# The old state of a gated linear attention joins the new product through an identity matmul on TensorE instead of an addition on VectorE

## The chip, the cores and the metric

The kernel runs on one core of a Trainium2 chip. The metric is the device time of one execution in microseconds (us); the number given is the median of several executions.

## What is computed

Three layers follow each other. The first is a gated linear attention with a 48 x 48 state for each of 4 x 8 heads over 768 positions. The second sends each of the 3072 tokens to one of eight experts, if its skip score is positive. The third is a three-way maximum of products and an output product.

```
for t in range(S):                       # S = 768, state is 48 x 48 for each head
    state = alpha[:, :, t, :, None] * state + einsum('bhd,bhe->bhde', k[:, :, t], v[:, :, t])
    y[:, :, t] = einsum('bhd,bhde->bhe', q[:, :, t], state)
...
x[do_compute] += gate * (relu(x @ w1[e]) @ w2[e])      # one expert e per token
...
out = max(x @ w1, x @ w2, x @ w3) @ w_out
```

Only the first layer is touched by the change.

## The kernel before

The first layer works on chunks of 128 positions: 4 batches of 6 chunks, 24 chunks in all, with all 8 heads of a batch at once (4 pairs of heads, two heads of a pair in the two halves of the 128 partitions). The loop at line 491 takes one chunk a pass; below, **step n** is its pass for chunk n, and c is the number of the chunk in its batch (0 to 5). The rest of the program (the experts and the third layer, from about 145 us on) follows the loop and is not changed.

One step holds, for TensorE (PE) in this order: `scores(n+1)` (line 265, 8 matmuls with operands of 64 partitions), `trans(n+1)` (line 256, 4 transposes), `rows(n-1)` (line 316, 4 matmuls), then `outs(n)`: 4 matmuls of the old state with the queries (line 303, tile `bd`, only for c > 0) and 8 of the masked scores with the values (line 306, a stationary operand of 64 columns); last `upd(n)` (line 283, 8 matmuls of keys and values with a stationary operand of 64 columns, tile `pu`). All are in float32, and each such matmul appears in the trace as two instructions. `trans` and `upd` do nothing for the last chunk of a batch (c = 5), so `trans` is missing in the step with c = 4 and `upd` in the step with c = 5.

VectorE (DVE) does in one step: two scans for chunk n+3 (lines 222 and 236, with a small reciprocal at 230 between them), two masks for chunk n+1 (line 271, tiles `ps` to `sm`), a small reduction of the logits of chunk n-1 (line 324), and the update of the state: `pu + w` (line 290, for c > 0) and the product with the decay (line 291; line 288 for c = 0), which writes the new `w`. After the last chunk of a batch come the routing instructions of that batch: lines 358 to 377 in the next step with c = 0, lines 390 to 413 two steps later.

ScalarE (ACT) then copies `w` into the block-diagonal `bd` (lines 294 and 295), which the next step's line 303 reads. GpSimd (POOL) multiplies keys and queries by the scans' results (lines 225 and 240) and issues the scatters of routed tokens (line 416); its order is fixed too. DMAs are issued by SyncE (SP).

Each engine runs its instructions in the order in which the program writes them. `ps`, `pu`, `py`, `px` and `pk` have one buffer each in PSUM (two tiles for `ps`), so `scores(n+2)` must wait for the masks of chunk n+1, and the update on VectorE must wait for the end of line 283 of its own step. Neither engine can therefore get a whole step ahead of the other.

Of the kernel before, what the change touches and what calls it, by code (L numbers as in the profile page):

```python
# [15 lines left out]
ALU = mybir.AluOpType  # L16
# [4 lines left out]
NP = H // 2  # L21
# [60 lines left out]
def tile_gla_moe_moe2(ctx, tc, akq, vp, rp, wgt, cst, io, ew, md, out):  # L82
    nc = tc.nc
    V, A, G, T, SY = nc.vector, nc.scalar, nc.gpsimd, nc.tensor, nc.sync
# [35 lines left out]
    with tc.manual_schedule():  # L120
        cs = const.tile([128, 3 * 128 + NTILE + 8], F32, name="cs")
        rps = const.tile([PR, NP, 105], F32, name="rps")
        ident = cs[:, 0:128]
# [125 lines left out]
        fr, kks, yts, wt, xr, lg = {}, {}, {}, {}, {}, {}  # L249
# [24 lines left out]
        def upd(j):  # L274
            b, c = seq[j]
            if c == NC - 1:
                return
            kk = kks.pop(j)
            pu = ps_u.tile([128, 512], F32, name="pu")[:, 0:NP * D].rearrange("p (a d) -> p a d", a=NP)
            for p in range(NP):  # L280
                for i in range(2):
                    r0 = 64 * i
                    T.matmul(pu[r0:r0 + 64, p, :], kk[:, p, r0:r0 + 64], vt[j][:, (2 * p + i) * D:(2 * p + i + 1) * D],
                             start=True, stop=True)
            w = wk.tile([PR, NP, D], F32, name="w")
            tb = totm[:, b, :, c + 1:c + 2].to_broadcast([PR, NP, D])
            if c == 0:
                V.tensor_tensor(w, pu, tb, ALU.mult)
            else:
                V.tensor_tensor(pu, pu, wt[b, c], ALU.add)  # L290
                V.tensor_tensor(w, pu, tb, ALU.mult)
            wt[b, c + 1] = w
            t = bd[(c + 1) % 2]
            A.copy(t[0:64, :, 0:D], w[0:64])
            A.copy(t[64:PR, :, 64:64 + D], w[64:PR])
# [195 lines left out]
        for n, (b, c) in enumerate(seq):  # L491
# [10 lines left out]
            low_part = rows(n - 1) if n else None  # L502
            outs(n)
            upd(n)
            if n > nseq - 4:
                low_part()
# [51 lines left out]
        for k in range(k3):  # L558
            for m in range(2):
                T.matmul(acc[k][:, m * 128:(m + 1) * 128], xe[:, m, k * 128:(k + 1) * 128], ident,  # L560
                         start=False, stop=False)
# [244 lines left out]
        tb = [big(f"tb{i}") for i in range(5)]  # L806
# [318 lines left out]
        for s in range(2):  # L1125
# [9 lines left out]
            for j in range(8):  # L1135
                if s == 1 and j == 7:
                    break
                n, c = 1 - j // 4, j % 4
# [226 lines left out]
```

## Time and profile before

| | |
|---|---|
| median of 3 executions | 592.22 us (592.09 to 594.73) |
| the profiled execution | 592.59 us, span 590.8 us |
| TensorE busy, matmuls | 563.1 us (95% of the span) |
| VectorE busy | 440.9 us (75%) |
| ScalarE busy | 297.8 us (50%) |
| GpSimd busy | 247.5 us (42%) |
| mean granted TensorE clock | 0.998 of 2.4 GHz |
| loop of the 24 chunks | from about 7 us to 135 us |

The span runs from the first to the last instruction; 1.8 us of the profiled execution's time lie around it. The shares are means over the whole program and hide the loop, in which VectorE is nearly as busy as TensorE. So the loop is read from its own stretches, from the waits in it, and from the order of instructions in time, whose rows give the start of a group, how long it lasts until its last instruction ends, and after a "<-" whom it waited for. A matmul takes longer from its start to its end than the next one needs to follow it, so prices of matmuls are read from one group's start to the next one's start.

### The profile page before, as it was taken

What the parts mean: (1) busy time and instruction counts of PE and PEld (TensorE: products, weight loads), DVE (VectorE), ACT (ScalarE), POOL (GpSimd) and SP (SyncE); (2) the same over time, 40 slices, a digit from 0 to 9 for tenths busy, and PEclk for the clock granted to TensorE, in tenths of its full rate; (3) what the DMA queues carried; (4) which work ended last, traced back from release to release, by engine and by line L of the source; (5) the groups of instructions that cost most, each with busy time, mean ns of one, the idle gap of its engine ahead of it and who ended that gap; (6) DMA issues with size and microseconds to landing.
All of it is one profiled execution on the core that took longest, in us unless ns stands there. A gap on an engine that the chain in (4) does not pass through costs nothing.

```text
span 590.8 us, 10710 instructions
## 1 busy us (share of the span) xinstructions
PE 563.1 (95%) x3995; PEld 502.8 (85%) x3995; DVE 440.9 (75%) x747; ACT 297.8 (50%) x602; POOL 247.5 (42%) x202
## 2 busy tenths in 40 slices
PE   6999999999999989999999998899999999999995
PEld 3888888888899989999988887788787899887895
DVE  7999999977788898888769895493766674766700
ACT  3656575654576665665333444355354375454310
POOL 5554598653365445654122022122364400455410
PEclk9999999999999999999999999999999999999999
DMA  8889898925787879884419149307464571355011
GB/s 314 323 252 340 288 305 312 347 97 186 255 276 281 303 227 329 260 306 153 161 35 287 37 153 373 144 11 283 138 234 163 199 256 53 134 199 202 0 56 59
DMA packets 50973, 123.04 MB, mean 208 GB/s; under 512 B 4546, under 2 KB 38832, under 8 KB 47328
## 3 DMA queue, kind: packets, MB, share of 16 engines
q1 hardware_dynamic: 44512, 112.13, 55.4%
q10 hardware_dynamic: 3840, 5.31, 2.6%
q0 software_dynamic: 2560, 4.83, 2.2%
q8 instruction: 33, 0.54, 0.4%
q14 instruction: 28, 0.23, 0.1%
HBM read 93.03 MB, written 32.28 MB: 212 GB/s over the span
## 4 chain that ended last, share of the span: by engine, by line
PE 55%; DVE 13%; issue 5%; ACT 4%; DMA 3%; POOL 1%; ACTq 0%; DVEq 0%; POOLq 0%
PE po L1001 3%; PE po L1002 3%; PE po L1003 3%; PE ph L1001 3%; PE ph L1002 3%; PE ph L1003 3%; PE ph L658 2%; PE ph L659 2%; PE po L678 2%; PE po L676 2%; PE po L677 2%; PE ph L660 2%; DVE wl L118 2%; DVE hf L855 2%; PE po L1071 2%
## 5 line engine op out<-in xcount | busy, mean ns | idle before, releaser
L118 POOL TENSOR_TENSOR wl<-raw,wh 128x768 fp32r<-128x768 f32 x26 | 49.2, 1893 | 63.9 <-ACT wh L117 63.8
L118 DVE TENSOR_TENSOR wl<-raw,wh 128x768 fp32r<-128x768 f32 x38 | 57.2, 1506 | 11.6 <-ACT wh L117 11.6
L117 ACT CAST wh<-raw 128x768 fp32r<-128x768 f32 x64 | 53.5, 836 | 21.8 <-PE po L678 10.7
L658 PE MATMUL ph<-xh,wh 128*128 128x256 f32 x192 | 56.5, 294 | 3.7 <-DVE hl L664 3.5
L659 PE MATMUL ph<-xl,wh 128*128 128x256 f32 x192 | 54.5, 284 | 0.4 <-DVE xl L118 0.3
L660 PE MATMUL ph<-xh,wl 128*128 128x256 f32 x192 | 54.4, 283 | 0.0
L676 PE MATMUL po<-wh,hh 128*128 128x384 f32 x128 | 43.5, 340 | 0.0
L678 PE MATMUL po<-wh,hl 128*128 128x384 f32 x128 | 43.3, 338 | 0.0
L677 PE MATMUL po<-wl,hh 128*128 128x384 f32 x128 | 43.2, 337 | 0.0
L658 PEld LDWEIGHTS ph<-xh,wh 128*128 128x128 f32 x192 | 36.5, 190 | 5.3 <-DVE hl L664 5.1
L265 PE MATMUL ps<-q,k 64*128 64x128 f32 x384 | 31.7, 286 | 9.3 <-POOL q L240 5.5
L225 POOL TENSOR_TENSOR k<-akq,sf 128x512 f32<-128x512 f32 x24 | 28.5, 1188 | 23.0 <-DVE sf L222 14.5
L265 PEld LDWEIGHTS ps<-q,k 64*128 64x128 f32 x384 | 26.0, 187 | 13.7 <-POOL q L240 6.9
L659 PEld LDWEIGHTS ph<-xl,wh 128*128 128x128 f32 x192 | 36.4, 190 | 0.8 <-DVE xl L118 0.8
L660 PEld LDWEIGHTS ph<-xh,wl 128*128 128x128 f32 x192 | 36.4, 189 | 0.0
L416 POOL DMA_INDIRECT slots<-xr,si x24 | 24.4, 1015 | 27.8 <-DVE xr L413 11.9
L664 DVE SCALAR_TENSOR_TENSOR hl<-ph,hh 128x256 fp32r<-128x256 f32 x64 | 26.5, 417 | 9.4 <-ACT hh L663 9.3
L663 ACT ACTIVATE hh<-ph 128x256 fp32r<-128x256 f32 x64 | 24.7, 386 | 14.9 <-PE ph L660 13.6
L236 DVE TENSOR_TENSOR_SCAN ap<-akq,pcs 128x521 f32<-128x521 f32 x24 | 29.8, 1241 | 2.2
L222 DVE TENSOR_TENSOR_SCAN sf<-akq,pcs 128x520 f32<-128x520 f32 x24 | 29.4, 1225 | 2.4 <-DMA akq<-in_akq_dram 2.1
L271 DVE TENSOR_TENSOR sm<-ps,cs 128x512 f32<-128x512 f32 x48 | 30.3, 674 | 0.5 <-PE ps L265 0.5
L240 POOL TENSOR_TENSOR q<-akq,ap 128x512 f32<-128x512 f32 x24 | 28.4, 1185 | 5.2 <-DVE ap L236 2.9
(659 smaller groups left out, 1722.3 us busy)
## 6 DMA issues: line engine op xcount, KB each, us to landing
raw<-in_ew_dram SPq DMA_DIRECT2D x15, 1536.0 KB, 6.8
akq<-in_akq_dram SPq DMA_DIRECT2D x22, 772.5 KB, 7.2
rm<-in_md_dram SPq DMA_DIRECT2D x12, 768.0 KB, 7.6
mh<-wd SPq DMA_DIRECT2D x7, 1024.0 KB, 5.1
ml<-wd SPq DMA_DIRECT2D x7, 896.0 KB, 6.7
raw<-wd SPq DMA_DIRECT2D x6, 1024.0 KB, 5.1
raw<-wd SPq DMA_DIRECT2D x6, 896.0 KB, 6.7
vt<-in_vp_dram SPq DMA_DIRECT2D x24, 200.0 KB, 7.0
```

Of the source, the lines that this page charges most:

```text
L117: A.copy(h, src)
L118: (eng or V).tensor_tensor(l, src, h.bitcast(F32), ALU.subtract)
L265: T.matmul(ps[i][:, p, :], kh[j][r0:r0 + 64, p, :], qh[j][r0:r0 + 64, p, :], start=True, stop=True)
L658: T.matmul(ph, wh[:, z], xh_[e][:, k, :], start=(k == 0), stop=False)
L659: T.matmul(ph, wh[:, z], xl_[e][:, k, :], start=False, stop=False)
L660: T.matmul(ph, wl[:, z], xh_[e][:, k, :], start=False, stop=(k == k3 - 1))
L676: T.matmul(po, hh[:, zm], wh, start=(f == 0), stop=False)
L677: T.matmul(po, hh[:, zm], wl, start=False, stop=False)
L678: T.matmul(po, hl[:, zm], wh, start=False, stop=(f == nf1 - 1))
L1001: T.matmul(bk, uh, vh, start=start, stop=False, skip_group_check=not start)
L1002: T.matmul(bk, uh, vl, stop=False, **more)
L1003: T.matmul(bk, ul, vh, stop=True, **more)
```

## The change

In `upd`, for c > 0, the old state `wt[b, c]` (128 partitions x 192 columns, float32) is multiplied by the 128 x 128 identity into `pu` first, with `start=True`. The eight products of keys and values then accumulate on it, each with `start=False`. VectorE's addition is left out; its product with the decay reads `pu` as before. Sixteen of the 24 steps have c from 1 to 4 and are changed; in the four steps with c = 0 and the four with c = 5 the same instructions run as before. No other instruction changes its place on any engine.

```diff
             pu = ps_u.tile([128, 512], F32, name="pu")[:, 0:NP * D].rearrange("p (a d) -> p a d", a=NP)
+            if c:
+                T.matmul(pu, ident, wt[b, c], start=True, stop=False)
             for p in range(NP):
                 for i in range(2):
                     r0 = 64 * i
                     T.matmul(pu[r0:r0 + 64, p, :], kk[:, p, r0:r0 + 64], vt[j][:, (2 * p + i) * D:(2 * p + i + 1) * D],
-                             start=True, stop=True)
+                             start=(c == 0), stop=(c == 0 or p == NP - 1))
             w = wk.tile([PR, NP, D], F32, name="w")
             tb = totm[:, b, :, c + 1:c + 2].to_broadcast([PR, NP, D])
-            if c == 0:
-                V.tensor_tensor(w, pu, tb, ALU.mult)
-            else:
-                V.tensor_tensor(pu, pu, wt[b, c], ALU.add)
-                V.tensor_tensor(w, pu, tb, ALU.mult)
+            V.tensor_tensor(w, pu, tb, ALU.mult)
             wt[b, c + 1] = w
```

## Rows read from the trace of the kernel before

**Rows 1.** Windows: busy us (x instructions) of PE, PEld, DVE, ACT, POOL; PEclk, DMA share, GB/s.

```profile
95.00:110.00 15.00, 14.55 (x187) 13.40 (x189) 14.40 (x28) 8.27 (x22) 13.31 (x13) 1.00 0.83 287
145.00:592.00 447.00, 430.11 (x2378) 384.68 (x2377) 313.92 (x460) 217.27 (x391) 160.59 (x109) 1.00 0.53 184
```

**Rows 2.** Waits, 14 to 131 us: line waited for, total us, times, longest us.

```profile
PE ps L265 <- DVE sm L271: 3.3, 5, 0.9
PE ps L265 <- POOL q L240: 1.5, 3, 0.7
...
DVE pu L290 <- PE pu L283: 4.1, 7, 1.3
```

**Rows 3.** Order in time, PE, steps 3 to 5: start us, length us, group.

```profile
27.39 1.16 PE L265 MATMUL ps<-q,k 64*128 64x128 f32 x16
...
28.97 1.04 PE L316 MATMUL px<-rps,yt 128*128 128x105 f32 x8
29.84 1.08 PE L303 MATMUL py<-q,bd 128*128 128x128 f32 x8
30.85 1.09 PE L306 MATMUL py<-sm,vt 128*64 128x128 f32 x16
31.77 0.62 PE L283 MATMUL pu<-vt,kk 128*64 128x48 f32 x16
32.33 1.16 PE L265 MATMUL ps<-q,k 64*128 64x128 f32 x16
33.42 1.14 PE L316 MATMUL px<-rps,yt 128*128 128x105 f32 x8
34.39 1.08 PE L303 MATMUL py<-q,bd 128*128 128x128 f32 x8
...
41.53 1.09 PE L306 MATMUL py<-sm,vt 128*64 128x128 f32 x16
42.55 1.25 PE L265 MATMUL ps<-q,k 64*128 64x128 f32 x16
```

**Rows 4.** Order in time, weight loads (PEld) of step 3.

```profile
30.85 0.85 PEld L306 LDWEIGHTS py<-sm,vt 128*64 128x64 f32 x16
31.67 0.60 PEld L283 LDWEIGHTS pu<-vt,kk 128*64 128x64 f32 x16
```

**Rows 5.** Order in time, PE: matmuls with wide moving operands after the loop.

```profile
139.29 0.61 PE L560 MATMUL pk<-cs,xe 128*128 128x128 f32 x4
139.74 0.61 PE L560 MATMUL pu<-cs,xe 128*128 128x128 f32 x4
...
201.19 0.34 PE L676 MATMUL po<-wh,hh 128*128 128x384 f32 x1
201.37 0.34 PE L677 MATMUL po<-wl,hh 128*128 128x384 f32 x1
```

**Rows 6.** Order in time, DVE: a step that DVE sets, and its parts.

```profile
95.77 0.19 DVE L324 TENSOR_REDUCE pcs<-px 128x9 f32<-128x36 f32 x1
95.87 0.35 DVE L290 TENSOR_TENSOR pu<-pu,w 128x192 f32<-128x192 f32 x1
96.26 0.36 DVE L291 TENSOR_TENSOR w<-pu,totm 128x192 f32<-128x192 f32 x1
...
100.42 0.20 DVE L324 TENSOR_REDUCE pcs<-px 128x9 f32<-128x36 f32 x1
```

**Rows 7.** Order in time, DVE: first and next instruction around both routing parts.

```profile
47.06 0.20 DVE L358 TENSOR_REDUCE mx<-pcs 128x6 f32<-128x48 f32 x1
...
48.98 1.21 DVE L222 TENSOR_TENSOR_SCAN sf<-akq,pcs 128x520 f32<-128x520 f32 x1
...
58.71 0.22 DVE L390 TENSOR_TENSOR rk<-pr,om 128x48 f32<-128x48 f32 x1
...
60.30 1.21 DVE L222 TENSOR_TENSOR_SCAN sf<-akq,pcs 128x520 f32<-128x520 f32 x1
```

**Rows 8.** The chain that ended last, at the end of the loop.

```profile
130.54 0.37 DVE w L291
```

## The prediction

> **What bounds the kernel now.** I read the windows first. After the loop TensorE is busy 430.11 of 447 us [rows 1], and its first work there needs the loop's last results, so whatever the loop loses or gains at its end is passed on in full. Inside the loop the two engines that the change touches are both almost full: 14.55 and 14.40 us of 15 [rows 1]. The granted clock is 1.00, the 2.4 GHz level, in all stretches; PE is busy enough that I expect no change there. Next come the waits: PE waits for VectorE's masks 5 times, 3.3 us in all, and 3 times for GpSimd's queries; VectorE waits 7 times for line 283, 4.1 us in all [rows 2]. So neither engine alone is the bound: they take turns, step by step, and the question is which one ends last in each step.
>
> TensorE's step, where it waits for nothing, is 32.33 - 27.39 = 4.94 us [rows 3]. VectorE's step, where it waits for nothing, is 100.42 - 95.77 = 4.65 us [rows 6]. So a plain step is set by TensorE. Two steps of each batch hold routing on VectorE, 48.98 - 47.06 = 1.92 us and 60.30 - 58.71 = 1.59 us [rows 7]; there VectorE needs 6.2 to 6.6 us and TensorE waits. Of the changed steps, c = 1 and c = 3 are the ones that follow the routing and start late for it; c = 2 and c = 4 are set by TensorE.
>
> **What the change removes.** Sixteen additions on VectorE, each 96.26 - 95.87 = 0.39 us from its start to the next start [rows 6], say 0.40 with the wait for its own result. VectorE's step falls from 4.65 to 4.25 us. This counts only where VectorE sets the step, and once at the very end, where the last `w` is on the chain that ended last [rows 8].
>
> **What it adds.** Sixteen identity matmuls of 192 float32 columns, two instructions each, between lines 306 and 283. The trace has no such matmul there, so I price its parts.
> - *The passes.* Four instructions with 128 float32 columns take 139.74 - 139.29 = 0.45 us [rows 5], 0.1125 each; 192 columns by proportion 0.169. One single-pass matmul of 384 columns takes 0.18 us [rows 5]. Two passes: 0.34 us (bounds 0.225, as if 128 columns, and 0.36).
> - *The change of shape.* Lines 306 and 283 both hold a stationary operand of 64 columns (128*64 in the rows); the identity is 128*128. Where 283 follows 306 it does so after 31.77 - 30.85 = 0.92 us; where another shape follows the same 16 instructions, it takes 42.55 - 41.53 = 1.02 [rows 3]. So leaving a shape costs 0.10 us. Entering one costs too: line 316 lasts 29.84 - 28.97 = 0.87 us to its successor after transposes of its own shape, but 34.39 - 33.42 = 0.97 after line 265, which has another [rows 3]. The weight loads say why: line 283's first load starts 0.10 us ahead of its matmul (31.67 against 31.77), line 306's, which follows a change, at the same time as its matmul (30.85 and 30.85) [rows 3, 4]. The identity changes the shape twice where there was no change: 0.10 to leave 306, 0.10 to enter with 128 columns, 0.10 to leave the identity, and some 0.03 to enter 283 with 64 columns (from 0 to 0.10).
> - *Sum:* 0.34 + 0.33 = 0.67 us. Bounds: 0.23 if the change of shape were free and the passes at their cheapest, 0.75 if all is at its dearest. I take 0.67, since each part has a near row.
>
> The Trainium skill, page "TensorEngine Tiling (Array Packing)", section "Tiling Modes" (Key Properties), says that changing the tiling mode drains TensorE. It speaks against this change. The trace agrees with 0.10 us for the drain, but shows a second part, the weight load that is not made ahead; with the drain alone an identity would cost 0.54 us and the sum below would come to +2.1 us instead of +3.2.
>
> Nothing else is added: the identity reads `w` of the step before, long written, and waits for nothing new. Accumulating costs nothing by itself, since line 306 does it already (in the 0.92 us above it accumulates on line 303). VectorE's scan now follows the product directly; if it had to wait for the logits' reduction itself, at most 0.09 us in VectorE's steps, 0.4 us in all.
>
> **The sum.** TensorE's changed step becomes 4.94 + 0.67 = 5.61 us, VectorE's 4.25.
> - *A batch with scans (the first three).* c = 1: hidden, VectorE with 1.92 us of routing needs 6.2. c = 2: +0.67 on the path. c = 3: TensorE's 0.67 is hidden behind the 1.59 us of routing, and VectorE, which sets this step, is shorter by its addition: -0.40. c = 4: +0.67. Net 2 x 0.67 - 0.40 = +0.94. (In the first batch there is no routing; there c = 2 and c = 3 pay and VectorE sets c = 4 with some extra copies. The net is the same.) Three of them: +2.82.
> - *The last batch.* Its scans have run out, so VectorE has room; c = 2, 3 and 4 all pay, and the last `w` comes 0.40 earlier: 3 x 0.67 - 0.40 = +1.61.
> - *What is taken up.* TensorE waited for GpSimd's queries 1.5 us in three places after the second batch, the last of 0.7 [rows 2]. A later TensorE uses the first two up: -0.8; the third gives nothing, since VectorE's routing of the same step starts from TensorE's end, not from GpSimd. The steps with c = 5 and 0 and the one after began some 0.13 us late for the masks; three times that is gone: -0.4.
>
> Together 2.82 + 1.61 - 1.2 = **+3.2 us**, or 9x - 2.8 with x the price of an identity above 0.5. From the profiled execution's 592.59 that gives 595.8. That execution lies 0.37 above the median of the runs, so against the median it is 592.22 + 3.2 = **595.4 us**.
>
> **Rivals.**
> 1. *The change of shape is free (not slower).* The weights are loaded beforehand and an identity costs its passes alone, 0.34 us. A batch then nets 2 x 0.34 - 0.40 = +0.28; two batches stay within GpSimd's 0.8, the third within the masks' 0.4, and only the last counts: 3 x 0.34 - 0.40 = +0.6, that is 592.8 us. It decides from x below 0.5. For it: the second pass and a stationary operand that is always the same. Against it: the four starts in [rows 3, 4]. The Trainium skill, page "TensorE: Matmul & The Clock Gate", section "Part 2: What happens when you issue a matmul", says that TensorE pulls a weight load ahead of running matmuls when the row groups differ or it goes to the background buffer; that rule would make this rival. The trace agrees for line 283 and not where the shape changes.
> 2. *VectorE is the bound everywhere (faster).* Then all 16 additions come off: 16 x 0.39 = 6.3 us, 585.9 us. Against it: VectorE itself waits 4.1 us for line 283 [rows 2], and its plain step is shorter than TensorE's. It would need an identity that fits into TensorE's waits in every step.
> 3. *Both weight loads stand bare.* If the second pass too waits for its load, about another 0.2 us by the two costs of a change above, x is near 0.9 and the sum 9 x 0.9 - 2.8 = +5.3: 597.5 us. For it: no row has two passes of this length after a change. Against it: within line 316 eight instructions follow each other at 0.11 us, loads included [rows 3].
>
> **How the numbers follow.** 0.5% of 592.2 is 3.0 us, about what a measurement of this kernel can tell from no change; the sum crosses it at x = 0.64. The forecast has a chance of 0.70; within its x from 0.54 to 0.75 the time is 594.3 to 596.6 us, with the scan's wait 597.0, and I give 0.42 to the part above 3.0 us and 0.28 to the part below. Rival 1 has 0.15 (same), rival 2 0.03 (faster), rival 3 0.09 (slower); 0.03 is left for a time that stays where it is for a reason I don't see (same). Faster 0.03, same 0.46, slower 0.51. The range from 592.7 to 597.1 us leaves out rival 2, most of rival 3 and the lower half of rival 1, about 0.18.
>
> **What would show it.** In the changed profile: from line 304 (306 before) to the identity 1.02 us instead of 0.92; from the identity to line 285 about 0.53; a weight load of the identity that starts with its matmul, not before; TensorE's plain step 5.6 us; VectorE's plain step 4.25 us and far longer waits of line 289 for `pu`; TensorE's waits for GpSimd's queries gone or smaller; no loss in the steps with c = 1. The identity and line 285 together lasting under 0.95 us would prove rival 1; an unchanged end of the loop near 130 us would too. I am wrong if the loop's end moves by something other than the identities, for example through the zero fills that hold GpSimd's first scatter.

## The result, and the profile after

The changed kernel took 596.50 us (median of 11 executions, 595.04 to 598.43) against 592.75 us (591.59 to 594.79) for the kernel before. The ratio is 1.0058, with a 95% interval from 1.0042 to 1.0075: slower by 0.6%, by the medians 3.75 us. The prediction was 595.4 us and slower by 3.2.

Where the time went is read in the loop of the 24 chunks. A good ruler is the product that writes `w` (line 291 before, 289 after): there are 20, five in a batch. From the first to the last it took 115.07 us before (15.47 to 130.54) and 118.45 us after (17.18 to 135.63): **+3.38 us**. The profiled execution of after was 4.1 us longer in its span; of the rest, +1.71 lies ahead of the first product, where the granted clock fell in this execution (last section), and -0.99 behind the last. The part behind the last product took 458.5 to 463.1 us in the 14 profiles of this document, so -0.99 is within its scatter.

One piece of the +3.38 us is scatter too. Between the fifth product of batch 2 and the first of batch 3 the profile of before took 9.04 us, because TensorE waited twice for GpSimd's queries; a second profile with the same loop (the warmed kernel before of the experiments, whose four batches agree with before within 0.02 us) waited less and took 8.46 us. Lines of before, then of the second:

```profile
69.45 1.16 PE L265 MATMUL ps<-q,k 64*128 64x128 f32 x16 [0.55 <-POOL q L240]
74.24 1.16 PE L265 MATMUL ps<-q,k 64*128 64x128 f32 x16 [0.23 <-POOL q L240]
```

```profile
73.67 1.16 PE L265 MATMUL ps<-q,k 64*128 64x128 f32 x16 [0.17 <-POOL q L240]
```

Against that profile's loop of 114.49 us the changed loop is 3.96 us longer. What happens inside the four batches does not scatter so, and is the safer reading.

TensorE in the plain step 3 of after, in time (start, length, group; the same step as in [rows 3]):

```profile
29.76 1.16 PE L265 MATMUL ps<-q,k 64*128 64x128 f32 x16
...
33.23 1.09 PE L304 MATMUL py<-sm,vt 128*64 128x128 f32 x16
34.25 0.59 PE L281 MATMUL pu<-w,cs 128*128 128x192 f32 x2
34.77 0.67 PE L285 MATMUL pu<-vt,kk 128*64 128x48 f32 x16
35.37 1.16 PE L265 MATMUL ps<-q,k 64*128 64x128 f32 x16
```

The step is 35.37 - 29.76 = 5.61 us long, 0.67 more than in [rows 3]. Line 304 is followed after 1.02 us, not 0.92; the identity (L281) takes 0.52 to the next group; line 285 takes 0.60 to the next scores, where it took 0.56. The weight loads (PEld) of the same step:

```profile
33.22 0.85 PEld L304 LDWEIGHTS py<-sm,vt 128*64 128x64 f32 x16
34.25 0.30 PEld L281 LDWEIGHTS pu<-w,cs 128*128 128x128 f32 x2 [0.17 <-DVE pcs L322]
34.77 0.55 PEld L285 LDWEIGHTS pu<-vt,kk 128*64 128x64 f32 x16 [0.23 <-issue]
```

Both L281 and L285 start to load when their matmuls start, at 34.25 and 34.77. In [rows 4] line 283 loaded 0.10 us ahead. VectorE's plain step is the distance of two reductions, 4.25 us, and its scan is not held up:

```profile
98.88 0.19 DVE L322 TENSOR_REDUCE pcs<-px 128x9 f32<-128x36 f32 x1
98.98 0.35 DVE L289 TENSOR_TENSOR w<-pu,totm 128x192 f32<-128x192 f32 x1
...
103.13 0.19 DVE L322 TENSOR_REDUCE pcs<-px 128x9 f32<-128x36 f32 x1
```

The waits of both engines from 14 to 131 us answer [rows 2] (line waited for: total us, times, longest). TensorE has none left for VectorE or GpSimd; VectorE waits 12.6 us for `pu`:

```profile
PE pr L185 <- issue: 0.2, 1, 0.2
```

```profile
DVE w L289 <- PE pu L285: 12.6, 10, 1.9
```

So TensorE is the nearly full engine of the loop of after. The windows from the first `w` product to TensorE's last work on `pu` say it in one line each (columns as in [rows 1]), before first, then after:

```profile
15.47:130.13 114.66, 109.44 (x1420) 99.77 (x1420) 104.17 (x219) 68.43 (x179) 73.73 (x69) 1.00 0.85 287
```

```profile
17.18:135.61 118.43, 118.21 (x1452) 103.39 (x1451) 99.02 (x204) 68.59 (x179) 74.64 (x70) 1.00 0.81 273
```

TensorE was idle 5.22 us there and is idle 0.22 us now. Sixteen identities at 0.67 are 10.7 us. They used up those 5.0 us, and the last `w` now follows TensorE 0.02 instead of 0.41 us later; with +3.38 as the result, some 1.9 us remain. Scores account for 1.27 of it: line 265 was busy 29.40 us in the first window and 28.13 in the second, with the same 352 instructions. I read that as waits inside the group, which count as busy. They are not all gone: in batch 2 the scores behind c = 1 and c = 3 still last 1.66 and 1.52 us instead of 1.16, so VectorE still sets these two steps. The other 0.7 us was not traced. The page of after has the busy times of the engines, and TensorE's share of the chain that ended last, which rose from 55% to 74%; ScalarE and GpSimd are as busy as before:

```profile
PE 573.5 (96%) x4026; PEld 507.7 (85%) x4027; DVE 435.3 (73%) x731; ACT 298.2 (50%) x602; POOL 248.0 (42%) x202
...
PE 74%; DVE 10%; issue 4%; DMA 4%; ACT 4%; POOL 1%; ACTq 0%; SPq 0%; DVEq 0%; POOLq 0%
```

Batch 4 shows both sides of the trade. The `w` products on VectorE, before:

```profile
109.40 0.36 DVE L288 TENSOR_TENSOR w<-pu,totm 128x192 f32<-128x192 f32 x1
115.96 0.36 DVE L291 TENSOR_TENSOR w<-pu,totm 128x192 f32<-128x192 f32 x1
121.05 0.36 DVE L291 TENSOR_TENSOR w<-pu,totm 128x192 f32<-128x192 f32 x1
126.00 0.36 DVE L291 TENSOR_TENSOR w<-pu,totm 128x192 f32<-128x192 f32 x1
130.54 0.36 DVE L291 TENSOR_TENSOR w<-pu,totm 128x192 f32<-128x192 f32 x1
```

and after:

```profile
112.87 0.36 DVE L289 TENSOR_TENSOR w<-pu,totm 128x192 f32<-128x192 f32 x1
119.03 0.35 DVE L289 TENSOR_TENSOR w<-pu,totm 128x192 f32<-128x192 f32 x1
124.80 0.36 DVE L289 TENSOR_TENSOR w<-pu,totm 128x192 f32<-128x192 f32 x1 [1.42 <-PE pu L285]
130.41 0.36 DVE L289 TENSOR_TENSOR w<-pu,totm 128x192 f32<-128x192 f32 x1 [1.90 <-PE pu L285]
135.63 0.36 DVE L289 TENSOR_TENSOR w<-pu,totm 128x192 f32<-128x192 f32 x1 [1.97 <-PE pu L285]
```

The intervals went from 6.56, 5.09, 4.95, 4.54 to 6.16, 5.77, 5.61, 5.22: -0.40 where `w` waits for nothing (VectorE sets the step), +0.66 to +0.68 where it waits for `pu` (TensorE sets it).

### The profile page after: what moved, and what is told of

Same layout as the page of the kernel before. It is cut to its first block, busy times and chain, and to the rows that moved or that the text cites. A ratio compares the mean times of both kernels' runs of the same rounds, so it can differ in the third digit from the quotient of the medians.

```text
span 594.9 us, 10746 instructions
## 1 busy us (share of the span) xinstructions
PE 573.5 (96%) x4026; PEld 507.7 (85%) x4027; DVE 435.3 (73%) x731; ACT 298.2 (50%) x602; POOL 248.0 (42%) x202
## 4 chain that ended last, share of the span: by engine, by line
PE 74%; DVE 10%; issue 4%; DMA 4%; ACT 4%; POOL 1%; ACTq 0%; SPq 0%; DVEq 0%; POOLq 0%
PE ps L265 5%; PE py L304 4%; PE po L999 3%; PE px L314 3%; PE po L1000 3%; PE po L1001 3%; PE py L301 3%; PE ph L999 3%; PE ph L1000 3%; PE ph L1001 3%; PE ph L656 3%; PE ph L657 2%; PE po L676 2%; PE po L674 2%; PE po L675 2%
## 5 line engine op out<-in xcount | busy, mean ns | idle before, releaser
L118 DVE TENSOR_TENSOR wl<-raw,wh 128x768 fp32r<-128x768 f32 x38 | 55.9, 1470 | 10.6 <-ACT wh L117 10.6
L661 ACT ACTIVATE hh<-ph 128x256 fp32r<-128x256 f32 x64 | 24.6, 384 | 14.1 <-PE ph L658 12.6
```

The source lines that it names most:

```text
L118: (eng or V).tensor_tensor(l, src, h.bitcast(F32), ALU.subtract)
```

## The experiments

The theory was that an identity costs 0.67 us of TensorE, half in its passes and half in two changes of tile shape, wherever TensorE sets the step. The rivals were that the shape is free, that both weight loads stand bare, that VectorE is the bound, and later that part of the loss has nothing to do with the steps. The times of this kernel's executions scatter by some 3 us and more, and they follow the mean granted clock of each (before, on the two undisturbed chips of the experiments, at 0.998: 591.4 to 592.4 us; at 0.992: 593.8 to 597.2). So each experiment is read first from its loop (first to last `w` product, and the steps in it) and only then from its median. "Loop" below is against the 115.07 us of before.

**Without the change of shape: identity in two halves of 64 columns.** The changed kernel, with an identity of the shape of its neighbours, as four instructions.

```diff
-                T.matmul(pu, ident, wt[b, c], start=True, stop=False)
+                for i in range(2):
+                    T.matmul(pu[64 * i:64 * i + 64], ident[:, 64 * i:64 * i + 64], wt[b, c], start=True, stop=False)
```

> The identity in two halves of 64 columns, one for each half of pu's partitions, so that the stationary operand has the same shape as lines 304 and 285 around it (128*64) and no change of shape is added; the arithmetic is the same. Theory (an identity of 0.67 us is 0.34 of passes and 0.33 of two changes of shape): a plain step of TensorE of 5.28 us instead of 5.61, weight loads ahead of their matmuls, loop end some 2.7 us earlier than with the change, 0.6 us above the kernel before. Rival (the passes and the added accumulation cost it, the shape costs nothing): plain step 5.6 us, time as with the change, +3.4 us. Second rival (two halves do not run side by side): plain step 5.6 or above.

```profile
31.08 1.09 PE L305 MATMUL py<-sm,vt 128*64 128x128 f32 x16
32.00 0.49 PE L282 MATMUL pu<-w,cs 128*64 128x192 f32 x4
32.33 0.62 PE L286 MATMUL pu<-vt,kk 128*64 128x48 f32 x16
32.88 1.16 PE L265 MATMUL ps<-q,k 64*128 64x128 f32 x16
```

```profile
31.89 0.25 PEld L282 LDWEIGHTS pu<-w,cs 128*64 128x64 f32 x4
```

TensorE in time: line 305 is followed after 0.92 us again, the identity takes 0.33, and the plain step is 5.27 us. The weight load starts 0.11 us ahead of its matmul. The price fell from 0.67 to 0.33. Loop +0.93, of which +0.38 lies in the batches. Time 595.63 us, ratio 1.0031 (1.0008 to 1.0054). That median is 2.3 us over before, more than the loop; in the profiled executions 1.8 us of the 2.6 between their spans lie behind the last product, in code that is the same.

**Without the change of shape: identity placed between matmuls of its own shape.** The changed kernel, with `pu` opened ahead of the old state's matmuls in `outs`.

```diff
             if c:
-                T.matmul(pu, ident, wt[b, c], start=True, stop=False)
+                pu = opened.pop(j)
+            else:
+                pu = state_tile()
...
             py = ps_y.tile([PR, NP, C], F32, name="py")
+            if c and c < NC - 1:
+                opened[j] = state_tile()
+                T.matmul(opened[j], ident, wt[seq[j]], start=True, stop=False)
             if c:
                 for p in range(NP):
```

> The same identity matmul of 128 columns as in the change, but issued ahead of the product of the old state with the queries (line 301 of the change), among matmuls of its own shape. Theory of the change of shape: no change of shape is added, plain step 5.28 us, time +0.6 us over the kernel before. Rival (the instruction itself is dear wherever it stands): plain step 5.6 us, time +3.4 us.

```profile
30.31 1.04 PE L323 MATMUL px<-rps,yt 128*128 128x105 f32 x8
31.19 0.51 PE L307 MATMUL pu<-w,cs 128*128 128x192 f32 x2
31.54 1.05 PE L310 MATMUL py<-q,bd 128*128 128x128 f32 x8
```

```profile
31.10 0.30 PEld L307 LDWEIGHTS pu<-w,cs 128*128 128x128 f32 x2
```

TensorE in time: the same instruction costs 0.35 us here instead of 0.52, with nothing lost before it, and its weight load starts 0.09 us ahead. The plain step is 5.26 us, the loop +0.67, of which +0.38 lies in the batches, as with the halves. Time 594.19 us, ratio 1.0015 (0.9993 to 1.0036). One kernel kept the place and changed the shape, the other kept the shape and changed the place, and both lost half of the price: it goes with the change of shape between neighbours. The Trainium skill, page "TensorE: Matmul & The Clock Gate", section "Part 2: What happens when you issue a matmul", has TensorE pull a weight load ahead of running matmuls where the row groups don't conflict or the load goes to the background buffer. Between equal shapes the trace agrees (0.09 us ahead here); across a change of shape the load started with its matmul (34.25 in the kernel after).

**Identity and addition together.** The kernel before, with an identity that the products overwrite.

```diff
+            if c:
+                T.matmul(pu, ident, wt[b, c], start=True, stop=True)
```

> The kernel before with the identity matmul added at the place of the change, its result overwritten by the products (start=True), and VectorE's addition kept: TensorE's side of the change alone. Theory (two engines that take turns): plain step of TensorE 5.61 us, VectorE's step 4.65 us; the time is above the change by what the additions were worth, +5.7 us over the kernel before, 2.4 us over the change. Rival (VectorE's additions were hidden and their removal is worth nothing but the last one): +3.4 to +3.8 us over the kernel before.

Plain step 5.61 us, loop +5.76; time 599.06 us, ratio 1.0082 (1.0059 to 1.0106). This is the identity's price without the addition's gain. The products overwrite the identity's result here and the plain step is the same 5.61 us, so accumulating on it costs nothing that shows.

**Neither.** The other corner: the addition is left out and no identity is put in.

```diff
-            if c == 0:
-                V.tensor_tensor(w, pu, tb, ALU.mult)
-            else:
-                V.tensor_tensor(pu, pu, wt[b, c], ALU.add)
-                V.tensor_tensor(w, pu, tb, ALU.mult)
+            V.tensor_tensor(w, pu, tb, ALU.mult)
```

> Left out: the old state is not added to the new product at all, neither by VectorE nor by TensorE, so the state of each chunk is that chunk's own product with its decay. It is what the change would give if the identity cost nothing. TensorE's plain step stays 4.94 us. Theory (only steps that VectorE sets get shorter, and what they gain is partly met again by TensorE's waits for GpSimd's queries): 1.1 us less from first to last state product than in the kernel before, 114.0 against 115.1. Rival (gain and price simply add: the kernel with both identity and addition is +5.8, the changed kernel +3.4, so the addition is worth 2.4): -2.4, 112.7. Third (VectorE sets all steps): -6.3.

With the two kernels this makes a square. The distances of `w` products, first to fifth in each batch, and from the fifth to the first of the next, in us:

| | before | after | identity and addition | neither |
|---|---|---|---|---|
| batch 1 | 22.95 | 23.74 | 24.30 | 22.41 |
| batch 2 | 22.56 | 23.11 | 23.92 | 21.77 |
| batch 3 | 22.58 | 23.13 | 24.17 | 21.81 |
| batch 4 | 21.14 | 22.76 | 23.16 | disturbed |
| between | 8.37, 9.04, 8.43 | 8.67, 8.52, 8.52 | 8.36, 8.49, 8.43 | 8.66, 9.67, 8.47 |

Inside the first two batches gain and price simply add: the identity costs 1.35 and 1.36 us (before to both), the addition gives back 0.56 and 0.81 with the identity (both to after) and 0.54 and 0.79 without it. In the third it is 0.77 without and 1.04 with the identity, where the kernel with both has 0.25 more than in batch 2 for no reason that I looked for. So the rival of additive parts holds in the steps. Up to the first product of batch 4 the kernel without either is at 92.79 us where before is at 93.93, that is -1.14: of 2.10 us gained in three batches 0.96 was given back between them. At the first border this is a rule: it took 8.55 to 8.67 us in the seven profiles without an addition at c = 4 and 8.36 or 8.37 in the seven with one, so what the last `w` of the batch gains is mostly lost again. The second border (9.67, +0.63) also varies between runs of one and the same kernel (9.04, 8.46 and, on a disturbed chip, 10.14), so that part stays open. With 0.40 for the last batch the whole comes to some -1.5, between the theory's -1.1 and the rival's -2.4, and does not decide between them. The last batch was disturbed on that chip (last section). Time 595.22 us where before took 598.76, ratio 0.9942 (0.9926 to 0.9959). By the trace the gain is 1.5 us (1.14, and 0.40 in the last batch as in the table's after against both), by the median 3.5 us with 4 executions on a chip that scatters; an identity that costs nothing would gain about as much, not more.

**The addition twice.** The kernel before with one more addition, into columns that nobody reads.

```diff
-            pu = ps_u.tile([128, 512], F32, name="pu")[:, 0:NP * D].rearrange("p (a d) -> p a d", a=NP)
+            pf = ps_u.tile([128, 512], F32, name="pu")
+            pu, pd = (pf[:, i * NP * D:(i + 1) * NP * D].rearrange("p (a d) -> p a d", a=NP) for i in range(2))
...
             else:
+                V.tensor_tensor(pd, pu, wt[b, c], ALU.add)
                 V.tensor_tensor(pu, pu, wt[b, c], ALU.add)
```

> The kernel before with VectorE's addition done twice (the first into unused columns of the same bank), no identity: VectorE's side alone, with the opposite sign. Theory: VectorE's step 5.05 us, now just above TensorE's 4.94, so that VectorE sets nearly every step; +3.3 us over the kernel before. Rival (VectorE's work is covered by TensorE): under +1 us. Rival (VectorE is the bound everywhere): 16 x 0.40 = +6.4 us.

Plain step 5.06 us, now set by VectorE; TensorE waited 4.8 us in 7 places for the masks; loop +4.45, 1.1 over the forecast (the batches +5.06, the second border -0.61). One step makes 1.2 of it, 98.13 to 104.42 us, 6.29 long against 5.05 for the same step of batch 2. TensorE had waited 1.16 us for a mask, and from 98.40 to 101.80 the granted clock was 0.57, which is mostly the 1.2 GHz level (windows, columns as in [rows 1]; PEclk is the third number from the end):

```profile
95.00:97.00 2.00, 0.84 (x23) 0.75 (x20) 2.00 (x3) 1.38 (x4) 1.69 (x3) 1.00 0.90 353
...
98.40:101.80 3.40, 3.40 (x18) 3.14 (x16) 3.26 (x6) 1.98 (x6) 2.92 (x4) 0.57 0.61 166
```

Time 597.75 us, ratio 1.0067 (1.0042 to 1.0091). An addition more costs the loop 4.45 us and an identity 5.76, so the kernel before stands near the point where both engines balance.

**The identity in half of the steps.** In c = 1 and 3 only (the diff), then in c = 2 and 4 only (with `on = c and c % 2 == 0`); the other steps add on VectorE.

```diff
-            if c:
+            on = c % 2
+            if on:
+                T.matmul(pu, ident, wt[b, c], start=True, stop=False)
...
+            if c and not on:
+                V.tensor_tensor(pu, pu, wt[b, c], ALU.add)
```

> The identity matmul opens the sum in steps c=1 and c=3 only; in steps c=2 and c=4 VectorE adds the old state as before. From the step lengths read in the traces of before and of the changed kernel (TensorE plain 4.94 with an add, 5.61 with an identity; VectorE plain 4.65 with an add, 4.25 without). Theory (an identity costs 0.67 us wherever TensorE sets the step, and a step pays back only what VectorE had made TensorE wait in it; the step c=1 comes in a stretch in which VectorE trails, so that half of the price is hidden): from first to last state product about +0.7 us against before, so some 592.9 to 593.9 where before is 592.5 to 593.2. Rival (the price is the same in every step, so half of the identities cost half of the whole +3.4): +1.7 us.

> The identity matmul opens the sum in steps c=2 and c=4 only; in steps c=1 and c=3 VectorE adds the old state as before. Theory (price is paid where TensorE sets the step, which it does in the later steps of a batch): from first to last state product about +2.25 us against before. Rival (same price in every step): +1.7 us. The two halves should add to about the whole change's +3.4 either way; what tells the two theories apart is whether this one costs about three times as much as the odd steps or as much.

Loop +1.17 for the odd steps (15.15 to 131.39), halfway between theory (0.7) and rival (1.7), and +2.59 for the even ones (16.71 to 134.37). By batches: odd +0.82, +0.01, +0.22, +0.68; even +0.70, +0.55, +0.54, +0.94. The batches add to +1.73 and +2.73; the second border took 0.56 and 0.52 off again, which by the scatter of that border may not be the identities' doing. Without the second border the odd steps cost +1.73, as the rival said, and the even ones +3.11, 1.8 times as much and not three times, so neither forecast holds for the whole. What holds is by batch: in batches 2 and 3, where routing makes VectorE late just then, the odd identities are nearly free; in batches 1 and 4 they are not, and I had counted the first batch wrong. Times 594.29 us (ratio 1.0018, 0.9994 to 1.0041) and 596.87 us (1.0043, 1.0023 to 1.0063). The two add to 3.76 against 3.38 for the whole.

**The identity twice.** A second one of the same shape ahead of the first.

```diff
             if c:
+                T.matmul(pu, ident, wt[b, c], start=True, stop=True)
                 T.matmul(pu, ident, wt[b, c], start=True, stop=False)
```

> The changed kernel with a second identity matmul of the same tile ahead of the first (overwritten by it), so the result is the same. Theory (of the 0.67 us of an identity 0.34 are the passes through the array and 0.33 the two changes of tile shape, which the pair pays once): plain step 5.61 + 0.34 = 5.95 us, from first to last state product +6.3 to +6.9 us against before (nine steps in which TensorE sets the pace, 9 x 1.01 - 2.8 = 6.3). Rival (the whole price lies with the instruction, not with the changes of shape): plain step 6.28 us, 9 x 1.34 - 2.8 = +9.3.

```profile
31.69 1.09 PE L305 MATMUL py<-sm,vt 128*64 128x128 f32 x16
32.72 0.59 PE L281 MATMUL pu<-w,cs 128*128 128x192 f32 x2
33.15 0.49 PE L282 MATMUL pu<-w,cs 128*128 128x192 f32 x2
33.57 0.67 PE L286 MATMUL pu<-vt,kk 128*64 128x48 f32 x16
```

TensorE in time: 305 to 286 takes 1.88 us where the changed kernel has 1.54, so the second identity costs 0.34, its passes alone. Plain step 5.94 us, loop 14.85 to 136.69, +6.77. Time 599.37 us, ratio 1.0102 (1.0084 to 1.0121). The two changes of shape are paid once a pair.

**A narrow identity.** Identity and addition together, the identity 16 columns wide.

```diff
+            if c:
+                T.matmul(pu[:, 0, 0:16], ident, wt[b, c][:, 0, 0:16], start=True, stop=True)
```

> The kernel before, with its additions, and one more identity matmul ahead of the products that is only 16 of the 192 columns wide and is overwritten by them. It measures the change of tile shape nearly alone. Theory (0.33 us of an identity's 0.67 is the change of shape and the rest goes with the columns): price 0.33 + 0.34 x 16/192 = 0.36 us, up to 0.45 if the second weight load is no longer covered by so short a pass; plain step 5.30 to 5.39 us, between the kernel with a full identity and an addition (5.61) and the kernel before (4.94); loop +2 to +3.2 us. Rival (the price goes with the columns alone): 0.06 us, plain step 5.00, loop under +0.5 us. Third (both weight loads bare for a short pass): about 0.6 us, plain step 5.5.

```profile
32.55 1.09 PE L308 MATMUL py<-sm,vt 128*64 128x128 f32 x16
33.57 0.40 PE L281 MATMUL pu<-w,cs 128*128 128x16 f32 x2
33.89 0.67 PE L285 MATMUL pu<-vt,kk 128*64 128x48 f32 x16
```

The plain step is 34.50 - 29.08 = 5.42 us, a price of 0.48: above the theory's 0.36 to 0.45, below the third case's 0.6. From the identity to the products it is 0.32 us, about the 0.30 us of its two weight loads. So 176 columns more cost only 0.19 us, and the price does not go with the columns. I read it as rival 3 of the prediction, real for narrow matmuls: the passes are too short to hide both loads. That is a reading; no run tells it from another cost that every identity has. Batches 1 and 3 took 23.89 and 23.52 us, +0.94 each, twice the price; batch 2 had one longer step that I did not follow up (c = 4, 6.27 us), and batch 4 was disturbed on that chip, so the forecast for the whole loop was not tried. Time 600.61 us where before took 598.76, ratio 1.0031 (1.0008 to 1.0054).

**TensorE kept busy at the start.** The first traces showed the granted clock falling between 12 and 18 us in some profiles, the changed kernel's among them. TensorE waits twice just before, near 6 to 8 and 10 to 12 us. The kernel before, with these waits filled by matmuls into an unused tile; then the same in the changed kernel, and beside it the first once more, on another chip:

```diff
-WARM = 15
+WARM = 21
...
         trans(0)
+        warm(7)
         prep(1)
```

> The kernel before with TensorE kept busy in its two gaps at the start: 21 warming matmuls ahead of the first scores where there were 15, and 7 more between the first transposes and the second scores. Theory (in some executions the granted clock falls to the lower level at 12 to 17 us because TensorE was idle in these gaps, which makes the second scores take 2.07 us instead of 1.16 and starts the chain of steps 1.7 us later): the fall at 12 to 17 us is gone in every trace, the first state product starts at about 15.4 us, the fastest time stays at 591.5 and the median comes 0.5 to 1 us nearer to it. Rival (the fall has nothing to do with the gaps): same scatter and median as before within 0.3 us, and the fall is still seen in some executions.

> The changed kernel with the same warming matmuls in TensorE's two gaps at the start as the warmed kernel before. Theory (the change costs what its steps cost, +3.4 us, and the fall of the clock at 12 to 17 us is a matter of its own that the warming takes away from both): no fall at 12 to 17 us, first to last state product 118.4 us as in the changed kernel, and 3.0 to 3.8 us over the warmed kernel before, so some 595.3 to 596.1. Rival (part of the +3.4 us is the fall, which the changed kernel meets more often): the two warmed kernels stand 2.5 us apart or less.

> The warmed kernel before once more, beside the warmed changed kernel. Theory: 592.3 us again, 0.8 to 1.6 us under the kernel before of the same call, lowest 590 to 591. Rival (the first gain was the scatter of the runs): within 0.5 us of the kernel before.

Windows of the changed kernel, then of the warmed kernel before:

```profile
9.00:12.00 3.00, 1.21 (x16) 0.85 (x12) 1.91 (x4) 1.40 (x4) 2.94 (x7) 1.00 1.03 413
12.00:15.00 3.00, 2.71 (x20) 2.48 (x20) 2.85 (x5) 0.00 (x0) 1.95 (x3) 0.56 1.04 411
```

```profile
9.00:12.00 3.00, 2.56 (x21) 1.34 (x17) 1.88 (x3) 1.40 (x4) 2.94 (x7) 1.00 1.03 414
12.00:15.00 3.00, 2.86 (x46) 2.58 (x48) 2.86 (x5) 1.08 (x3) 1.97 (x3) 1.00 1.04 409
```

PEclk is 0.56 against 1.00 from 12 to 15 us. The warmed kernel before took 592.28 us where before took 593.63, ratio 0.9968 (0.9949 to 0.9987), and on the other chip 596.35 against 598.73, ratio 0.9965 (0.9951 to 0.9978). **It is the fastest version here that computes the same, 0.3% under the kernel before.** The warmed changed kernel took 599.07 us, 2.72 above it: between the theory's 3.0 and the rival's 2.5, so this pair does not decide how often the fall of the clock added to the first comparison. Both traces were disturbed in batch 4; over batches 1 to 3 the warmed changed kernel has 70.20 us and the warmed kernel before of the same chip 68.14, +2.06, where the pair without warming has 69.98 - 68.09 = +1.89.

## Why the prediction was right, point by point

- **The price of an identity: right.** 0.67 us was forecast and 0.67 measured, with its parts: 1.02 us to leave line 306 (304), 0.52 to line 285, 0.60 from there to the next scores. The identity in halves (0.33) and the doubled one (+0.34) confirm the split between passes and shape. Rivals 1 and 3 fall for this size. The Trainium skill's rule that a change of tiling mode drains TensorE ("TensorEngine Tiling (Array Packing)", "Tiling Modes") has the right sign, and the trace shows the 0.10 us at line 304; alone it would have given 0.54 us an identity by the prediction's parts, not 0.67. That the remaining 0.13 us is the weight loads is argued from their starts (with the matmul across a change of shape, 0.09 to 0.11 us ahead without one); no run separates the two parts.
- **TensorE sets c = 2, 3, 4 in the last batch and two steps in the others: right.** The kernel with both has +1.35, +1.36, +1.59 and +2.02 in the four batches; twice 0.67 is 1.34 and three times is 2.01. That is the 9x of the sum, but for 0.25 us more in batch 3.
- **The gain of the addition inside a batch: too small.** I gave -0.40 a batch. Measured against 2x, 2x, 2x and 3x it was -0.55, -0.79, -0.79 and -0.39, since c = 1, called hidden and put at zero, is a step that VectorE sets: its interval fell from 6.55 to 6.16 us in batch 2. The prediction had both numbers (VectorE needs 6.2 to 6.6 us there) and gave the gain to c = 3 alone. In the first batch c = 4 gave back 0.15, not 0.40. The batches together cost +3.51 us, not +4.43.
- **What is taken up between the batches: too large.** I gave 0.8 for GpSimd's queries and 0.4 for the masks. The three borders changed by +0.30, -0.52 and +0.09, together -0.13. The waits for queries and masks did vanish from TensorE's list, but the first and third borders got no shorter, and the second got shorter by the same half microsecond in an unchanged loop (8.46 us in the warmed kernel before).
- These two misses, -0.92 and +1.07, cancel: 9x - 2.65 = +3.38 measured, 9x - 2.8 = +3.2 forecast. The sum came out right to 0.2 us; the split of its minus term was not right, and the agreement is partly luck. Against the loop of the warmed kernel before the borders changed by +0.30, +0.06 and +0.09, the misses are -0.92 and +1.65, and the loop is +3.96: the forecast is then 0.8 too small. The medians (+3.75) lie between the two. The direction and the price of an identity hold against either.
- **Rival 2 (VectorE everywhere, -6.3): wrong.** Even without any identity the loop got only 1.1 us shorter by the start of batch 4.
- **The clock, which I expected not to change: wrong for the start.** In the profiled execution of after it fell at 12 to 15 us, and the first product came 1.7 us later. Whether this is why the medians moved by 3.75 us and the loop by 3.38 is not shown.
- **The range's upper end** mixes two starting points: 596.6 is the profiled 592.59 plus 9 x 0.75 - 2.8, and from the median 592.22 that the forecast and the lower end use it would be 596.2.

## What to carry to other kernels

Before moving work to an engine, ask which engine sets each step; in a loop in which two engines take turns, the receiving one pays in its own steps and the relieved one gains only in others. Here the 0.4 us of an addition came back in seven of sixteen steps, in one of them only in part (2.5 us in all), while 0.67 us was charged in nine. A single matmul of another tile shape between equal neighbours cost about as much again as its passes here (192 float32 columns), so put it next to matmuls of its own shape: that alone took the loop's loss from 3.4 to 0.7 us. And where a gain is a few tenths of a microsecond a step, compare the steps: a border between batches that moves by 0.6 us from run to run hides it.

## What I had not expected of the hardware

**Waits of TensorE can cost twice.** Of 11 profiles without the extra warming, 5 show a granted clock of 0.50 to 0.69 from 12 to 15 us, behind the two waits at the start, and of 3 with it none. Three are few; that the waits bring it on rests as much on the two ratios of the warmed kernel before. In the changed kernel it made the second scores take 2.07 instead of 1.16 us:

```profile
12.29 2.07 PE L265 MATMUL ps<-q,k 64*128 64x128 f32 x16 [2.08 <-POOL q L240]
```

and the loop started 1.71 us later (0.17 of it was there before the fall: the first scores began at 8.46 instead of 8.29 us). TensorE's busy time does not foretell it: from 9 to 12 us it was 0.91 both in profiles with the fall and without. Why the warmed kernel's fastest time (590.22 us against 591.44) is lower too is not settled; its second border was 8.46 us instead of 9.04.

**Some chips stall in one place.** On the chips of the last two groups of runs (both kernels with warming in one, the two without the old state or with the narrow identity in the other) before took 598.7 us, and near 118 to 134 us several engines stood still for some microseconds, and the profile names no releaser that fits (line 290 does not read `px`). VectorE of the warmed kernel before, in its second run:

```profile
129.25 0.37 DVE L290 TENSOR_TENSOR pu<-pu,w 128x192 f32<-128x192 f32 x1 [3.77 <-PE px L316]
...
133.55 1.29 DVE L271 TENSOR_TENSOR sm<-ps,cs 128x512 f32<-128x512 f32 x2 [3.08 <-remote]
```

The two `w` products around it stand 7.50 us apart there (122.15 and 129.65), and 4.94 us in the first run of the same kernel (120.48 and 125.42). What it is was not tested; it strikes both kernels. Each ratio here is taken on one chip; the loops are all set against one profile of before, so disturbed batches are left out of them where the text says so.
